# Size classes at the entry of an expert visit, and second products moved behind the join, in a fused attention and mixture-of-experts kernel

## The chip, the cores and the metric

One core of one Trainium2 chip runs the whole program. The metric is the device time of one execution in microseconds; the runs of a kernel are summed up by their median. Five engines work at once, each through its own list of instructions: TensorE (PE in the profile, with its weight loads as PEld), VectorE (DVE), ScalarE (ACT), GpSimd (POOL) and SyncE (SP), which issues DMA. An `If` in the program is a comparison and a branch in the list of every engine.

## The reference

Attention with rotary positions, a gated MLP behind an RMS norm, and then the stage that this change is about, an expert layer that sends each of 2304 tokens to one of 8 experts:

```python
def _moe2_ref(x, modality_id, w_gate, modality_bias, w1, w2):
    logits = x @ w_gate + modality_bias[modality_id]
    e_idx = np.argmax(logits, axis=1)
    ...                                  # probs: softmax of logits
    gate_w = probs[np.arange(N), e_idx]
    out = np.zeros((N, D), dtype=np.float32)
    for e in range(E):
        mask = e_idx == e
        if not mask.any():
            continue
        h = np.maximum(x[mask] @ w1[e], 0.0)
        out[mask] = gate_w[mask, None] * (h @ w2[e])
    return out.astype(np.float32)
```

D is 512, and the hidden width F is 1024. How many tokens an expert gets is known only when the kernel runs.

## The kernel before

Attention and MLP take the first 850 us or so and are not touched. The expert stage is a list of visits. A visit is one expert and up to 384 of its tokens (`VT`); an expert with more gets a further visit. Visit 0 is the fullest expert and is always laid out for 384 tokens, without a branch. Visits 1 to 5 always run, and 6 to 13 stand in nested `If`s on the number of visits (`nvis`); here there are eight visits, 0 to 7. What a visit is (expert, column of the table of tokens, size) VectorE works out while visit 0 runs: `count1` writes the size of visit 1 (`vn1`), `visits` the rest (`vi`). `number` loads such a value into registers, for the size on all engines.

`body` branches on the size: first above 256 or not, then above 288 and above 352, or above 128. Each of the five leaves is a whole visit for 128, 256, 288, 352 or 384 tokens, and after it the engines join and go on with the next visit's load and comparisons. By the column counts in the trace, visits 1 to 7 run as 288, 256, 256, 384, 352, 128 and 352.

A leaf (`visit`, in steps that it yields) makes, for each of eight slices f of the hidden width, 12 products over the transposed tokens `xT` (three for each of four pieces of w1, since values are held as a high and a low part) into one of three banks `ph`; ScalarE applies ReLU into the high part of `hq`, and VectorE subtracts to get the low part. Then come the second products, for each tile of 128 tokens in two halves of 12, into a bank `po`; VectorE scales the tile by its gate into `cvt` (`put`), and GpSimd scatters it to `out`. `small_visit`, for up to 128 tokens, makes the hidden values with tokens as rows in two halves of 12 products, and turns them by transposes (`turn`).

`ahead`, called after each step, puts two kinds of work for the next visit between these: `xT` (four TensorE transposes of a gathered tile of tokens into a bank `pt` or `pc`, a ScalarE cast for the high part, a VectorE subtraction for the low) at the steps that `TURNS` names, and `wsplit` (a weight piece of 512 KB, already loaded by SP, cast by ScalarE and split by VectorE) at the steps that `SPLITS` names; an entry s: n means that after step s all pieces up to 8v + n are split. A visit uses eight pieces, and there are eleven buffers `W`/`Wl`, so that a piece's split waits until the piece eleven before it is used up. `gather` fetches the next visit's tokens by an indirect DMA at the start of a visit. All this is written out in the order in which the engines run it; nothing reorders it later.

Of the kernel before, what the change touches and what calls it, by code (L numbers as in the profile page):

```python
# [9 lines left out]
F32 = mybir.dt.float32  # L10
# [40 lines left out]
class Kernel:  # L51
# [817 lines left out]
YW = 520  # L869
SPLITS = [  # L870
# [4 lines left out]
]  # L875
TURNS = [{}, {8: (0, 1), 9: (2,)}, {8: (0,), 9: (1, 2)}, {8: (0,), 9: (1,), 10: (2,)}]
# [22 lines left out]
class Fused(Kernel):  # L899
# [241 lines left out]
    def count1(self):  # L1141

        V = self.nc.vector
        r = self.rt
        c = r.tile([1, NE], F32, name="c1")
        V.tensor_tensor(c, self.cnt[0:1], self.oh1[0:1], op=ALU.mult)
        n = r.tile([1, 1], F32, name="n1")
        V.tensor_reduce(n, c, axis=AX.X, op=ALU.add)
        self.vn1 = r.tile([1, 1], I32, name="vn1")
        V.tensor_scalar(self.vn1, n, float(VT), None, op0=ALU.min)  # L1150

    def visits(self):
# [52 lines left out]
        V.tensor_scalar(vi[:, 2 * n1:3 * n1], col, 0.0, float(VT), op0=ALU.max, op1=ALU.min)  # L1205


    def moe_open(self):
# [10 lines left out]
        self.rawp, self.wpc, self.ev = {}, {}, {}  # L1219
# [18 lines left out]
    def number(self, v, x, **kw):  # L1238

        n1 = NV - 2  # L1240
        if v < 2:
            t = self.vn1 if x == 2 else self.vi0[0:1, 2 * v + x:2 * v + x + 1]
        else:
            t = self.vi[0:1, n1 * x + v - 2:n1 * x + v - 1]
        return self.nc.values_load(t, min_val=0, max_val=(NE - 1, 141, VT)[x], **kw)
# [62 lines left out]
    def visit(self, v, N):  # L1308
# [19 lines left out]
        for t0 in range(0, N, P):  # L1328
            ps = self.p_o()
            for x in range(2):  # L1330
                self.second(v, ps, x, t0, min(N - t0, P))
                if x == 1:
                    self.put(ps, ix, g, t0 // P, min(N - t0, P))
                yield s
                s += 1

    def small_visit(self, v):
# [28 lines left out]
        ps = self.p_o()  # L1366
        self.second(v, ps, 0, 0, P)
        turn(1)
        yield 8
        yield 9  # L1370
        self.second(v, ps, 1, 0, P)
        self.put(ps, ix, g, 0, P)
        yield 10
        yield 11
# [27 lines left out]
    def ahead(self, v, s, nt=3):  # L1402

        if s >= 8 and v + 1 < NV:
            for t in TURNS[nt].get(s, ()):
                self.xT(v + 1, t, self.p_h if nt == 1 and t == 2 else None)
        i = SPLITS[nt if v else 0]
        if s in i:
            self.wsplit(8 * v + i[s])
# [11 lines left out]
    def body(self, v, n, sizes):  # L1421

        if len(sizes) > 1:
            s = self.state()
            m = len(sizes) // 2
            with self.tc.If(n > sizes[m - 1]) as cmp:  # L1426
                self.body(v, n, sizes[m:])
            self.restore(s)
            with cmp.Else():
                self.body(v, n, sizes[:m])  # L1430
            return
        N = sizes[0]
        if N == P and v + 1 < NV:
            self.gather(v + 1)
        for s in self.visit(v, N) if N > P else self.small_visit(v):
            if s == 0 and N > P and v + 1 < NV:
                self.gather(v + 1)
            self.ahead(v, s, (N + P - 1) // P)

    def moe(self, v):  # L1440
        if v == NV:
            return
        with ExitStack() as es:
# [4 lines left out]
            n = self.number(v, 2)  # L1448
            self.body(v, n, SIZES)
            if v + 1 == NSTAT:  # L1450
                self.nvis = self.nc.values_load(self.vi[0:1, 3 * NV - 6:3 * NV - 5], min_val=2, max_val=NV)
            if v >= NSTAT:
# [15 lines left out]
    def run(self):  # L1468
# [72 lines left out]
        for s in self.visit(0, VT):  # L1541
# [61 lines left out]
```

## Time and profile before

| | |
|---|---|
| runs of the kernel before | 1141.26, 1143.42, 1147.27 us, median 1143.42 |
| the profiled execution | 1141.17 us, of which the profile's span is 1139.4 |
| TensorE busy | 1049.5 us, 92% of the span |
| VectorE, ScalarE, GpSimd busy | 657.6 us (58%), 459.5 (40%), 292.1 (26%) |
| granted TensorE clock, mean | 0.98 |

Times within the span are in us from its start. A busy time of TensorE is the union of its products' intervals; each product is preceded by a weight load that may overlap the product before it. [...] Idle time in brackets is what the engine waited before the row, and for whom; "issue" is time in which it waited for nothing that the profile shows. Rows named PEldq are those of TensorE's sequencer (loads of registers, comparisons and branches), and are not counted as busy.

### The profile page before, as it was taken

Reading aid. Unit: us, or ns where it says so; the run is one execution under the profiler, and the core shown is the slowest. Engines: PE = TensorE matmul, PEld = TensorE weight load, DVE = VectorE, ACT = ScalarE, POOL = GpSimd, SP = SyncE. Lnnn points to the kernel's source line nnn. Section 1 sums busy time; section 2 is a strip of 40 time slices with the busy share of each in tenths; the row PEclk is TensorE's granted clock in tenths of the full one; section 3 lists DMA queues with packets and bytes.
Section 4 is the critical chain, followed back from the end, with each engine's and each line's share of the span. In section 5 each row is a group of like instructions: output and inputs, shape, how many; then the busy total and the mean of one; then the engine's idle time right before and its main releaser. Section 6 shows DMA issues by size and latency. Waiting matters only on the chain. (4 is left out here: it accounts for less than half of the span.)

```text
span 1139.4 us, 19259 instructions
## 1 busy us (share of the span) xinstructions
PE 1049.5 (92%) x7174; PEld 893.3 (78%) x7174; DVE 657.6 (58%) x1308; ACT 459.5 (40%) x1024; POOL 292.1 (26%) x357
## 2 busy tenths in 40 slices
PE   3999999999999899999999999999988879998695
PEld 3776777676776688899999999998877768997583
DVE  8654656676544766556565564553477745663373
ACT  2655555565556333322222222221335434443252
POOL 7553446366302402112011110110010311221211
PEclk9999999999999899999999999999999999999897
DMA  4333344444230201111131111101064755654563
GB/s 131 95 85 89 103 109 130 108 105 129 59 89 24 77 19 58 54 47 47 40 122 47 38 47 47 38 10 56 30 216 156 229 176 169 202 171 140 168 223 122
DMA packets 75993, 114.05 MB, mean 100 GB/s; under 512 B 18536, under 2 KB 43392, under 8 KB 75842
## 3 DMA queue, kind: packets, MB, share of 16 engines
q1 hardware_dynamic: 72162, 100.25, 29.4%
q0 software_dynamic: 3680, 11.91, 3.1%
q8 instruction: 80, 1.31, 0.5%
q14 instruction: 71, 0.58, 0.2%
HBM read 85.91 MB, written 12.17 MB: 86 GB/s over the span
## 5 line engine op out<-in xcount | busy, mean ns | idle before, releaser
L760 PE MATMUL gv<-xh,whi 128*128 128x384 f32 x576 | 197.4, 343 | 1.8 <-ACT xh L738 1.4
L760 PE MATMUL gv<-xl,whi 128*128 128x384 f32 x576 | 195.2, 339 | 3.3 <-POOL xl L742 3.1
L760 PE MATMUL gv<-xh,wlo 128*128 128x384 f32 x576 | 195.2, 339 | 0.4 <-POOL wlo L659 0.4
L293 DVE TENSOR_REDUCE m<-s 128x1 fp32r<-128x576 f32 (+1 forms) x160 | 119.9, 752 | 123.2 <-PE s L292 122.0
L320 ACT ACTIVATE E<-sT 128x576 f32<-128x576 f32 (+1 forms) x160 | 105.0, 659 | 137.9 <-PE sT L319 132.5
L659 POOL TENSOR_TENSOR wlo<-cvt,whi 128x256 fp32r<-128x256 f32 x66 | 50.8, 773 | 339.9 <-ACT whi L658 339.8
L770 DVE TENSOR_TENSOR s<-s,gv 128x384 f32<-128x384 f32 x72 | 39.8, 554 | 154.4 <-PE gv L760 143.6
L760 PEld LDWEIGHTS gv<-xh,whi 128*128 128x128 f32 x576 | 108.9, 189 | 7.9 <-issue 3.5
L760 PEld LDWEIGHTS gv<-xl,whi 128*128 128x128 f32 x576 | 109.2, 190 | 5.4 <-POOL xl L742 3.4
L769 ACT ACTIVATE s<-gv 128x384 f32<-128x384 f32 x72 | 34.9, 492 | 189.6 <-PE gv L760 189.6
L760 PEld LDWEIGHTS gv<-xh,wlo 128*128 128x128 f32 x576 | 109.2, 190 | 1.2 <-POOL wlo L659 1.0
L317 PE MATMUL sT<-qT,kT 128*128 128x288 f32 (+1 forms) x320 | 79.7, 331 | 12.5 <-ACT qT L274 12.4
L788 PE MATMUL yps<-whi,hh 128*128 128x512 f32 x216 | 87.3, 404 | 2.9 <-ACT yacc L793 1.4
L331 PE MATMUL av<-E,vraw 128*64 128x288 f32 x640 | 86.2, 413 | 0.1
L803 DVE TENSOR_TENSOR yacc<-yacc,yps 128x512 f32<-128x512 f32 x99 | 67.6, 685 | 31.9 <-PE yps L788 30.7
L788 PE MATMUL yps<-wlo,hh 128*128 128x512 f32 x216 | 85.3, 395 | 0.0
L788 PE MATMUL yps<-whi,hl 128*128 128x512 f32 x216 | 85.2, 394 | 0.0
L292 PE MATMUL s<-kT,qT 128*128 128x288 f32 (+1 forms) x320 | 78.3, 330 | 6.1 <-DVE m L293 3.8
L1293 POOL DMA_INDIRECT x<-ysc,ix x27 | 32.9, 1218 | 151.2 <-DVE e L1127 76.2
L317 PEld LDWEIGHTS sT<-qT,kT 128*128 128x128 f32 (+1 forms) x320 | 47.9, 181 | 29.3 <-ACT qT L274 20.4
L319 PE MATMUL sT<-qB,kB 65*128 65x288 f32 (+1 forms) x320 | 69.8, 300 | 0.0
L331 PEld LDWEIGHTS av<-E,vraw 128*64 128x64 f32 x640 | 42.7, 137 | 31.6 <-issue 6.5
(288 smaller groups left out, 1979.0 us busy)
## 6 DMA issues: line engine op xcount, KB each, us to landing
raw<-in_w SPq DMA_DIRECT2D x52, 512.0 KB
stt<-in_w SPq DMA_DIRECT2D x26, 512.0 KB
stt<-in_w_gate SPq DMA_DIRECT2D x24, 256.0 KB
stt<-in_w_val SPq DMA_DIRECT2D x24, 256.0 KB
stt<-in_w_out SPq DMA_DIRECT2D x24, 256.0 KB
kB<-kT SPq DMA_DIRECT2D x32, 144.0 KB
qB<-qT SPq DMA_DIRECT2D x32, 144.0 KB
qT<-qT SPq DMA_DIRECT2D x32, 144.0 KB
```

What stands on the lines that cost most here:

```text
L292: nc.tensor.matmul(s[:n, u, 0:288], qA[:, j * 128:j * 128 + n], kA[:, u * 288:u * 288 + 288], start=True, stop=True)
L293: nc.vector.tensor_reduce(m[:n, j:j + 1], s[:n, :, 0:288], axis=AX.XY, op=ALU.max)
L317: nc.tensor.matmul(s[:n, u, 0:288], kA[:, j * 128:j * 128 + n], qA[:, u * 288:u * 288 + 288], start=True, stop=False)
L319: nc.tensor.matmul(s[:n, u, 0:288], kB[0:65, j * 128:j * 128 + n], qB[0:65, u * 288:u * 288 + 288], start=False, stop=True)
L320: nc.scalar.activation(e.rearrange("p (u c) -> p u c", u=2), s[:n, :, 0:288], AF.Exp, scale=0.125)
L331: self.nc.tensor.matmul(av[64 * h:64 * h + 64, 0:288], V[:, h, j * 64:j * 64 + 64], E[:, h if j < 4 else 0, j, 288 * u:288 * u + 288], sta ...
L659: nc.gpsimd.tensor_tensor(lo, f, fr(hi), op=ALU.subtract)
L760: nc.tensor.matmul(t[:, :CH], w[:, k], r[:, k], start=(n == 0), stop=(n == 11))
L769: nc.scalar.activation(s, ps[0][:, :CH], AF.Silu)
L770: nc.vector.tensor_tensor(s, s, ps[1][:, :CH], op=ALU.mult)
L788: nc.tensor.matmul(ps, l, r[:, 2], start=(n == 0), stop=(n == tot - 1))
L803: nc.vector.tensor_tensor(old[:, t], old[:, t], ps, op=ALU.add)
```

## The change

The two parts are these. First, the size is replaced by a class from 0 to 4, which `size_class` makes with one comparison for each of 128, 256, 288 and 352 and adds up; the class of the next visit is loaded at the start of a visit (`size`). `body` compares the class with 3, 2, 1 and 0 in a chain whose next link directly follows, and whose last fall-through is the leaf for 128 tokens; the other leaves are reached by a taken branch. Second, a leaf no longer holds the second products of the first token tile. They stand in `tail`, once, behind the join, together with the three transpositions of the next visit's tokens and two of its weight splits. `SPLITS` and `TURNS` are fitted to that: every leaf ends with the pieces up to 8v + 13 split, the tail brings 14 and 15, and piece 16 falls to the next visit's first step. Visit 0 keeps its order (`SPLIT0`, `first` = 0).

```diff
@@ -867,13 +867,14 @@
+SPLIT0 = {1: 7, 3: 8, 5: 9, 7: 10, 8: 11, 9: 12, 10: 13, 11: 14, 12: 15, 13: 16}
 SPLITS = [
...
-    {1: 9, 3: 10, 5: 11, 8: 12, 9: 13, 10: 14, 11: 15, 12: 16},
+    {},
+    {0: 9, 5: 11, 9: 13},
+    {0: 8, 1: 9, 3: 10, 5: 11, 8: 12, 9: 13},
+    {0: 8, 1: 9, 3: 10, 5: 11, 8: 12, 10: 13},
 ]
-TURNS = [{}, {8: (0, 1), 9: (2,)}, {8: (0,), 9: (1, 2)}, {8: (0,), 9: (1,), 10: (2,)}]
+TURNS = {8: (0,), 9: (1,), 10: (2,)}
@@ -1147,7 +1148,15 @@
-        V.tensor_scalar(self.vn1, n, float(VT), None, op0=ALU.min)
+        self.size_class(self.vn1, n, r.tile([1, 1], F32, name="sc1"))
+
+    def size_class(self, o, n, t):
+
+        V = self.nc.vector
+        V.tensor_scalar(t, n, float(SIZES[0]), None, op0=ALU.is_gt)
+        for x in SIZES[1:-2]:
+            V.scalar_tensor_tensor(t, n, float(x), t, op0=ALU.is_gt, op1=ALU.add)
+        V.scalar_tensor_tensor(o, n, float(SIZES[-2]), t, op0=ALU.is_gt, op1=ALU.add)
@@ -1202,7 +1211,7 @@
-        V.tensor_scalar(vi[:, 2 * n1:3 * n1], col, 0.0, float(VT), op0=ALU.max, op1=ALU.min)
+        self.size_class(vi[:, 2 * n1:3 * n1], col, r.tile([1, n1], F32, name="sc2"))
@@ -1325,7 +1334,8 @@
         s = 8
-        for t0 in range(0, N, P):
+        st["last", v] = ix, g
+        for t0 in range(first, N, P):
@@ -1363,15 +1373,26 @@
-        ps = self.p_o()
-        self.second(v, ps, 0, 0, P)
         turn(1)
+        st["last", v] = ix, g
         yield 8
         yield 9
+
+    def tail(self, v):
+
+        ix, g = self.st.pop(("last", v))
+        ps = self.p_o()
+        more = v + 1 < NV
+        if more:
+            self.xT(v + 1, 0)
+            self.wsplit(8 * v + 14)
+            self.xT(v + 1, 1)
+        self.second(v, ps, 0, 0, P)
+        if more:
+            self.xT(v + 1, 2)
+            self.wsplit(8 * v + 15)
         self.second(v, ps, 1, 0, P)
         self.put(ps, ix, g, 0, P)
-        yield 10
-        yield 11
@@ -1418,24 +1439,35 @@
-    def body(self, v, n, sizes):
...
+    def size(self, v):
+        if v not in self.cls:
+            self.cls[v] = self.number(v, 2)
+        return self.cls[v]
+
+    def body(self, v):
+
+        s = self.state()
+
+        def arm(x):
+            N = SIZES[x]
...
+        def choose(x):
+            if x == 0:
+                arm(0)
+                return
+            with self.tc.If(self.size(v) > x - 1, preferred_fallthrough_block=False) as cmp:
+                arm(x)
             self.restore(s)
             with cmp.Else():
-                self.body(v, n, sizes[:m])
...
+                choose(x - 1)
+
+        choose(len(SIZES) - 1)
@@ -1445,10 +1477,12 @@
-            n = self.number(v, 2)
-            self.body(v, n, SIZES)
+            for x in range(v, min(v + 2, NV)):
+                self.size(x)
+            self.body(v)
             if v + 1 == NSTAT:
                 self.nvis = self.nc.values_load(self.vi[0:1, 3 * NV - 6:3 * NV - 5], min_val=2, max_val=NV)
+            self.tail(v)
```

How this lies on the engines is seen best at the entry of visit 1 and at the join behind it. In these rows a line number, an operation, its output and inputs by tile (with buffer numbers) and its shape follow each other; `vn` and `vi` are the sizes, `po` the banks of second products, `ph` those of the first, `W` and `Wl` weight pieces. TensorE's list at the entry of visit 1, before:

```order
L1394 MATMUL po_8984<-Wl_8966,hq 128x512 x6
L1245 TENSOR_LOAD vn_9184
L1426 COMPARE_AND_BRANCH x3
L1319 MATMUL ph_8982<-xT,Wl_8967 128x384 x3
L1319 MATMUL ph_8982<-xT,Wl_8968 128x384 x3
```

and now, where four comparisons stand in a row, the sizes of two visits are loaded, and the leaf for 128 tokens follows instead of that for 384:

```order
L1415 MATMUL po_8984<-Wl_8966,hq 128x512 x6
L1254 TENSOR_LOAD vn_9184
L1254 TENSOR_LOAD vi
L1464 COMPARE_AND_BRANCH x4
L1367 MATMUL po_8985<-Wl_8967,xT 128x512 x3
L1367 MATMUL po_8985<-Wl_8968,xT 128x512 x3
```

At the join of visit 1, TensorE's list before goes from a leaf's last second product straight to the load and the comparisons:

```order
L1394 MATMUL po_8984<-W_8654,hq 128x512
L1426 UNCONDITIONAL_BRANCH
L1245 TENSOR_LOAD vi
L1426 COMPARE_AND_BRANCH x3
L1319 MATMUL ph_8982<-xT,Wl_8964 128x384 x3
```

Now the tail stands between the join and them: the transposes (L1312) of the next visit's tokens, and the second products of the first tile around the last of these:

```order
L1312 MATMUL pt_6361<-idf,x_8664 128x128 x4
L1415 MATMUL po_8984<-W_8651,hq 128x512 x6
L1415 MATMUL po_8984<-W_8652,hq 128x512 x6
L1312 MATMUL pc_6362<-idf,x_8665 128x128 x4
L1415 MATMUL po_8984<-W_8653,hq 128x512 x6
L1415 MATMUL po_8984<-W_8654,hq 128x512
L1415 MATMUL po_8984<-W_8655,hq 128x512
L1415 MATMUL po_8984<-W_8654,hq 128x512 x2
L1415 MATMUL po_8984<-W_8655,hq 128x512
L1415 MATMUL po_8984<-W_8654,hq 128x512
L1254 TENSOR_LOAD vi
L1464 COMPARE_AND_BRANCH x4
```

ScalarE's list at the same join, before, at the end of the leaf for 256 tokens: casts of the next visit's tokens (L1305) and of weight pieces (L1277) take turns, and all of them are in the leaf.

```order
L1305 CAST xT<-pc_6362 128x4x128
L1277 CAST Wl_8967<-raw_8647 128x1024
L1277 CAST Wl_8968<-raw_8648 128x1024
L1305 CAST xT<-pt_6361 128x4x128
L1305 CAST xT<-pc_6362 128x4x128
L1277 CAST Wl_8969<-raw_8649 128x1024
L1277 CAST W_8650<-stt 128x1024
L1277 CAST W_8651<-stt 128x1024
L1426 UNCONDITIONAL_BRANCH
```

Now the three casts of tokens (L1314) and two of weight pieces (L1286) have moved behind the branch, and the last piece has gone to the next visit:

```order
L1286 CAST Wl_8967<-raw_8647 128x1024
L1286 CAST Wl_8968<-raw_8648 128x1024
L1464 UNCONDITIONAL_BRANCH
L1314 CAST xT<-pc_6362 128x4x128
L1286 CAST Wl_8969<-raw_8649 128x1024
L1314 CAST xT<-pt_6361 128x4x128
L1314 CAST xT<-pc_6362 128x4x128
L1286 CAST W_8650<-stt 128x1024
L1254 TENSOR_LOAD vi
L1464 COMPARE_AND_BRANCH x4
```

## Rows read from the trace of the kernel before

**Rows 1.** TensorE in time: start, us, operation, out and in, shape, count, [idle].

```profile
886.57 0.66 PE L1303 MATMUL pt<-idf,x 128*128 128x128 f32 x4 [2.67 <-DMA x<-ysc,ix]
...
902.49 1.45 PE L1319 MATMUL ph<-xT,Wl 128*128 128x288 f32 x9 [0.71 <-issue]
...
939.08 6.18 PE L1319 MATMUL ph<-xT,Wl 128*128 128x256 f32 x34 [5.78 <-issue]
...
967.27 0.98 PE L1319 MATMUL ph<-xT,W 128*128 128x256 f32 x3 [2.27 <-issue]
...
992.60 0.69 PE L1319 MATMUL ph<-xT,Wl 128*128 128x384 f32 x3
...
1031.30 0.91 PE L1319 MATMUL ph<-xT,Wl 128*128 128x352 f32 x4 [4.08 <-issue]
...
1076.07 1.19 PE L1357 MATMUL po<-W,xT 128*128 128x512 f32 x2 [9.62 <-issue]
```

**Rows 2.** Branches of TensorE's sequencer (L1426): count, min/median/max ns, first and last start.

```profile
L1426 PEldq COMPARE_BRANCH  x2: 92/2107/4122, 898.2 to 898.3; - x2
...
L1426 PEldq COMPARE_BRANCH  x1: 4360/4360/4360, 929.0 to 929.0; - x1
...
L1426 PEldq COMPARE_BRANCH  x1: 4957/4957/4957, 933.8 to 933.8; - x1
...
L1426 PEldq COMPARE_BRANCH  x2: 306/2852/5399, 960.8 to 961.6; - x2
...
L1426 PEldq COMPARE_BRANCH  x1: 3725/3725/3725, 1027.5 to 1027.5; - x1
...
L1426 PEldq COMPARE_BRANCH  x2: 3303/4287/5271, 1067.3 to 1072.6; - x2
...
L1426 PEldq COMPARE_BRANCH  x1: 347/347/347, 1089.5 to 1089.5; - x1
```

**Rows 3.** The load of a size on TensorE's sequencer (L1245), same columns.

```profile
L1245 PEldq TENSOR_LOAD <-vi x1: 312/312/312, 933.4 to 933.4; - x1
```

**Rows 4.** TensorE in time, the last products of visit 1 and of visit 6.

```profile
924.40 0.60 PE L1303 MATMUL pc<-idf,x 128*128 128x128 f32 x4
924.75 8.55 PE L1394 MATMUL po<-W,hq 128*128 128x512 f32 x36
...
1089.74 1.53 PE L1394 MATMUL po<-W,hq 128*128 128x512 f32 x6
```

**Rows 5.** TensorE's comparison with the number of visits, behind visit 6 (L1443).

```profile
L1443 PEldq COMPARE_BRANCH  x1: 70/70/70, 1088.7 to 1088.7; - x1
```

**Rows 6.** Stretches: length, busy us of PE, PEld, DVE, ACT, POOL, PEclk, DMA, GB/s.

```profile
885.00:889.00 4.00, 2.43 (x13) 2.10 (x14) 2.07 (x7) 1.54 (x2) 1.55 (x1) 1.00 0.81 287
936.60:943.20 6.60, 4.12 (x19) 4.15 (x20) 0.42 (x1) 0.38 (x1) 0.00 (x0) 0.50 0.05 9
967.30:970.50 3.20, 3.20 (x15) 3.20 (x16) 0.00 (x0) 0.16 (x1) 1.00 (x1) 0.50 0.86 312
1032.20:1035.40 3.20, 3.20 (x13) 3.20 (x12) 0.27 (x1) 0.46 (x1) 0.00 (x0) 0.50 0.04 13
1069.70:1079.80 10.10, 3.73 (x9) 2.99 (x10) 1.50 (x3) 0.00 (x0) 3.67 (x4) 0.50 0.46 152
```

**Rows 7.** VectorE in time: the last operation that writes the sizes.

```profile
897.79 0.16 DVE L1205 TENSOR_SCALAR vi<-col 1x12 int32<-1x12 f32 x1
```

**Rows 8.** ScalarE in time, in visit 6: a weight piece, then the second ReLU.

```profile
1084.15 1.06 ACT L1277 CAST W<-stt 128x1024 fp32r<-128x1024 f32 x1
1085.10 0.60 ACT L1362 ACTIVATE x<-po 128x512 f32<-128x512 f32 x1
```

**Rows 9.** ScalarE's casts of tokens (L1305): count, min/median/max ns, first and last start.

```profile
L1305 ACT CAST xT<-pc x13: 586/587/596, 918.7 to 1117.4; 128x512 fp32r<-128x512 f32 x13
```

**Rows 10.** VectorE in time: the last scaling of a tile.

```profile
1125.64 0.75 DVE L1398 TENSOR_SCALAR cvt<-po,g 96x512 f32<-96x512 f32 x1 [1.84 <-PE po L1394]
```

**Rows 11.** GpSimd in time: the last scatter.

```profile
1129.09 0.92 POOL L1400 DMA_INDIRECT out<-cvt,ix  x1 [6.22 <-DMA out<-cvt,ix]
```

More of the change, by code (lines that the diff above doesn't have):

```diff
@@ L1218, in moe_open @@
         self.g_x = Ring(m, 3, [P, YW], F32, "x")
-        self.rawp, self.wpc, self.ev = {}, {}, {}
+        self.rawp, self.wpc, self.ev, self.cls = {}, {}, {}, {}
         self.nld = self.nsp = 0
@@ L1244, in number @@
             t = self.vi[0:1, n1 * x + v - 2:n1 * x + v - 1]
-        return self.nc.values_load(t, min_val=0, max_val=(NE - 1, 141, VT)[x], **kw)
+        return self.nc.values_load(t, min_val=0, max_val=(NE - 1, 141, len(SIZES) - 1)[x], **kw)
     def expert(self, v):
@@ L1306, in xT, with visit @@
         nc.vector.tensor_tensor(l, ps, fr(h), op=ALU.subtract)
-    def visit(self, v, N):
+    def visit(self, v, N, first=P):
         nc, st = self.nc, self.st
@@ L1402, in ahead @@
     def ahead(self, v, s, nt=3):
[L1404 to L1407, printed above, removed]
+        if v == 0 and s >= 8:
+            for t in TURNS.get(s, ()):
+                self.xT(1, t)
+        i = SPLITS[nt] if v else SPLIT0
         if s in i:
@@ L1419, in restore @@
         self.nld, self.nsp = s[4:]
-    def body(self, v, n, sizes):
[L1423 to L1427, printed above, removed]
+    def size(self, v):
[6 more added lines that the diff above has]
+            N = SIZES[x]
+            if N == P and v + 1 < NV:
+                self.gather(v + 1)
+            for y in self.visit(v, N) if N > P else self.small_visit(v):
+                if y == 0 and N > P and v + 1 < NV:
+                    self.gather(v + 1)
+                self.ahead(v, y, (N + P - 1) // P)
+        def choose(x):
[4 more added lines that the diff above has]
+                arm(x)
             self.restore(s)
             with cmp.Else():
-                self.body(v, n, sizes[:m])
[L1431 to L1438, printed above, removed]
+                choose(x - 1)
+        choose(len(SIZES) - 1)
     def moe(self, v):
@@ L1540, in run @@
         self.wsplit(6)
-        for s in self.visit(0, VT):
+        for s in self.visit(0, VT, 0):
             if self.rq:
```

3 rows, old and new, of the table SPLITS are left out of this document.

## The prediction

> **What bounds the kernel now.** I read the page's shares first, then TensorE's own order of time over the expert visits, then what its sequencer did in the holes, then the granted clock there. TensorE is busy for most of the span, so only its idle time and its slow time are worth anything, and of both the expert visits hold nearly all that a change of branches can touch. Visit 0 has a fixed size; by the column counts of the products, the seven visits behind it run as 288, 256, 256, 384, 352, 128 and 352 tokens. [Rows 1] show the first product of six of them (from 902.49 on), and the idle time before it: 0.71, 5.78, 2.27, none, 4.08 and 9.62 us. The releaser is "issue": nothing that the profile shows was being waited for. The seventh (352) waits only for VectorE, which I leave out. The sum is 22.46 us.
>
> The sequencer's branches say what it was [rows 2]. A comparison that falls through takes 0.09 us (0.13 with the gap behind it, an estimate), a jump to near code 0.31 or 0.35, and a jump to far code 3.3 to 5.4. The same jump, over the 384 arm into the 352 arm, took 3.73 us at 1027.5 and 0.35 at 1089.5; the first came just after another far jump, the second after a long straight run. So what is near depends on what has been fetched, not on the distance alone. The seven far jumps shown take 4.12, 4.36, 4.96, 5.40, 3.73, 3.30 and 5.27 us, a mean of 4.4. Before the jump stands the load of the size, 0.31 us and about 0.1 around it [rows 3].
>
> TensorE does not stop when its sequencer does. The exit branch of visit 1 began at 929.0, while the last 36 products ran from 924.75 to 933.30 [rows 2, 4]: the sequencer was 4.3 us ahead, some 18 products of 0.2375 us (8.55 / 36). Such a lead pays for one far jump, not for two. This is the pattern of [rows 1]: no jump, no idle; one, 0.71 or 2.27; two, 4.08 or 5.78; three (128 tokens), 9.62.
>
> The clock makes it dearer. [...] A wait of 2.67 us at 886.57 (for a gather) left it at 1.00 [rows 1, 6].
>
> So the visits lose 22.5 + 7.1 = 29.6 us, and the last one is followed by a wait on POOL.
>
> **The change, part by part.** The order shows that the change does what it says: a visit now costs TensorE one far jump in and at most one out, with 24 products and 12 transposes standing between the two. Those are 24 x 0.2375 + 12 x 0.09 = 6.8 us of work (four transposes start 0.35 us before what follows them [rows 4]), and no product is added or dropped.
>
> *Jumps out.* A lead of 4.3 us stands against 4.4: 0.2 us per miss. By the lengths of the arms (242 to 289 instructions of TensorE, a product being two) the arms of 256 and 288 come out onto near code, so three exits miss (384, 352, 352): 0.6 us. The small arm's exit is below.
>
> *Jumps in.* Behind the join, the queue holds at best the last 18 entries: 12 products, 4 transposes, 2 products, 12 x 0.2375 + 0.35 + 0.45 = 3.6 us. Against it stand the load of a size 0.41 (now that of the next visit, but still on the path), the comparisons that fall through at 0.13 each, the jump 4.4 and 0.05 until the first product. The two visits of 256 tokens (three comparisons fall through): 0.41 + 0.39 + 4.4 + 0.05 - 3.6 = 1.65 us each. The visits of 352 (one falls through; the last also tests the count of visits): 1.4 and 1.5. 384 tokens: its arm begins 70 instructions behind the first comparison, near code, 0.35 us, hidden. 128 tokens: falls straight in, hidden.
>
> *Visit 1* gets worse. It has no second products ahead of it (visit 0 keeps its order), and all engines now also load the size of visit 2, which VectorE finishes at 897.95 [rows 7]. The class adds four tiny operations there, and four for visit 1 earlier; at the 0.16 us of that row plus a gap, 0.8 us. So the load can start at 898.75, ends at 899.2, two comparisons 0.26, the jump 4.4: first product at 903.9. TensorE ran dry at 902.49 - 0.71 = 901.78: 2.1 us, where it lost 0.71.
>
> *The small visit (128)* gets a new wait. Its hidden tiles are turned by transposes that need the second ReLU. Today 12 second products stand before the second turn and cover it; now they are in the tail. The ReLU starts directly behind a weight cast of 1.06 us and takes 0.60 [rows 8]: 1.66 us in which TensorE has nothing. The jump out is 4.4 us but starts while the first products are still queued, so I take it as hidden behind this. The next visit's gather had the hole of 9.62 us to land in; now its rows are wanted some 9 us after the visit begins: 0.8 us more. Together 2.5, between 0 and 6.9 (2.5 with the whole jump behind it).
>
> *Moved casts.* The next visit's tokens are transposed, cast and split in the tail instead of between second products. The last transposes start some 3.2 us before the tail ends (twelve products and themselves), the cast takes 0.59 [rows 9] and VectorE's subtraction about as much, and the cast of a weight piece (1.06) stands before it. I price it at nothing: this slack covers it, and if the cover is gone it is a rival below. The weight splits are the same eight per visit; two stand in the tail. SP's loads follow the splits as before.
>
> *The end.* The last copy to `cvt` starts at 1125.64 but its scatter only at 1129.09, held by the landing of the scatter before [rows 10, 11]. After the change that one has the tail's 6.8 us to land. The 3.45 us between the two shrink to 2 at best about 1; I take 1.5 us gained.
>
> *Clock.* Six idle times of 1.4 to 2.5 us are left. 2.27 us brought the low clock once, 2.67 did not; half of six at 1.65 us: 5 us.
>
> **Sum.** After: 0.6 + 2 x 1.65 + 1.4 + 1.5 + 2.1 + 2.5 = 11.4, and 5 for the clock, 16.4 us. Saved: 29.6 - 16.4 + 1.5 = 14.7. The profiled execution took 1141.17 us, so 1126.5; the median of the runs, 1143.42, lies 2.25 above that execution, so 1128.7. I say 1128.5.
>
> [...]
>
> **Rivals.**
> *B: the queue hides the jumps in wholly.* If the lead behind the join is over 5.3 us, the jumps in cost nothing. Left are visit 1 (2.1), the small visit (2.5) and one low clock (1.65): 6.3; saved 29.6 - 6.3 + 1.5 = 24.8: 1118.5. For it: an exit that nearly vanishes, 0.71 at visit 1. Against it: every lead that I can read is 4.3 or less. [...] [Rows 4] show 4.3.
> *C: the queue is not full again by the end of the tail.* The small visit's sequencer left at 1088.7 while its products ran to 1089.74 + 1.53 = 1091.27 [rows 4, 5]: 2.6 us ahead only. With that, each of four jumps in costs 1.0 more, and all six idle times bring the low clock: 15.4 + 9.9 = 25.3; saved 5.8: 1137.6.
> *D: slower.* If the sequencer stands still at the tail's transposes until TensorE reaches them, there is no lead behind the join. The jumps in then cost 3.6 more each (20.6), the small visit's exit is open too (6.9), with 2.7 for visit 1 and the exits 30.2, and six low clocks at 1.9 make 41.6: 12.0 more than today, less the 1.5 of the end: 1153.9. It turns to the slow side where the lead is under about 1.2 us. For it: 2.6 us at the small visit. Against: elsewhere 4.3, past many waiting products.
> *E: the casts end last.* If ScalarE or VectorE enter the tail late, each visit starts some 1.5 us later: six of them, 9 us of the forecast's gain given back: 1137.5. For it: they do a whole visit's eight splits in less time. Against: at none of the six entries of [rows 1] are they what is waited for.
>
> **Chances.** Forecast 0.53, B 0.12, C 0.17, D 0.06, E 0.12. Half a per cent, 5.7 us, is about what a measurement of this kernel tells from no change, so faster means under 1137.7: nearly all of the forecast's share, all of B, half of C and E: 0.77. Within: 0.17. Slower: D, 0.06. The range for 8 in 10 goes from 1116 (B, with shorter jumps) to 1141 (C and E).
>
> **What would show it.** In the new trace: one far branch of about 4.4 us at each entry but those of 384 and 128, with 1 to 2.5 us idle behind it; at visit 1 more idle than the 0.71; nothing like 9.62 before 128 tokens, but a wait for the ReLU and a gather inside that visit; the clock at 0.50 in fewer stretches. Idle over 3 us at the entries of 256 would make C or D right; the first product of a visit waiting for VectorE or ScalarE would make E right.

## The result, and the profile after

The changed kernel takes 1131.33 us (median of 4 runs, 1129.5 to 1134.08), the kernel before 1142.35 on the same chip (4 runs). The ratio, here and below that of the means, is 0.9897, with a 95% interval from 0.986 to 0.9935. A second set of 6 runs, beside other kernels, gave 0.9912 (0.9889 to 0.9935). The profiled execution took 1130.2 us, with a span of 1128.4.

TensorE in time in the changed kernel, the rows that answer to [rows 1]; the idle time stands in brackets:

```profile
903.39 1.47 PE L1328 MATMUL ph<-xT,Wl 128*128 128x288 f32 x9 [1.07 <-issue]
...
937.28 2.85 PE L1328 MATMUL ph<-xT,Wl 128*128 128x256 f32 x22 [2.61 <-issue]
941.06 7.19 PE L1328 MATMUL ph<-xT,Wl 128*128 128x256 f32 x59 [0.93 <-issue]
...
965.38 1.31 PE L1328 MATMUL ph<-xT,W 128*128 128x256 f32 x9 [2.96 <-issue]
...
1026.27 6.03 PE L1328 MATMUL ph<-xT,Wl 128*128 128x352 f32 x36 [1.81 <-issue]
...
1067.43 0.66 PE L1357 MATMUL ph<-idf,x 128*128 128x128 f32 x4 [1.71 <-ACT x L1372]
1073.53 1.08 PE L1312 MATMUL pt<-idf,x 128*128 128x128 f32 x4 [5.44 <-issue]
...
1082.75 9.56 PE L1328 MATMUL ph<-xT,W 128*128 128x352 f32 x58 [0.72 <-issue]
```

The 9.62 us before 128 tokens are gone and the entries are down to 0.7 to 3 us. But inside the small visit there are now 1.71 us for the ReLU and, behind its second turn (the four transposes of its second half of hidden values), a hole of 5.44 that no visit had before. With 0.17 us at 907.14 the idle time of visits 1 to 7 is 17.4 us, where it was 23.0 (22.46, and the 0.54 before visit 7).

The branches of TensorE's sequencer (L1464), which answer to [rows 2], in the same columns; entries, with the exits of visits 4 (1013.3), 5 (1048.6) and 6 (1067.4):

```profile
L1464 PEldq COMPARE_BRANCH  x2: 64/2743/5422, 931.6 to 931.7; - x2
L1464 PEldq COMPARE_BRANCH  x2: 64/2934/5805, 959.3 to 959.4; - x2
L1464 PEldq COMPARE_BRANCH  x1: 358/358/358, 986.1 to 986.1; - x1
L1464 PEldq COMPARE_BRANCH  x1: 3847/3847/3847, 1013.3 to 1013.3; - x1
L1464 PEldq COMPARE_BRANCH  x2: 81/2556/5032, 1021.0 to 1021.2; - x2
L1464 PEldq COMPARE_BRANCH  x1: 3278/3278/3278, 1048.6 to 1048.6; - x1
L1464 PEldq COMPARE_BRANCH  x4: 64/64/72, 1056.5 to 1056.8; - x4
L1464 PEldq COMPARE_BRANCH  x1: 5924/5924/5924, 1067.4 to 1067.4; - x1
L1464 PEldq COMPARE_BRANCH  x1: 3841/3841/3841, 1078.9 to 1078.9; - x1
```

The far jumps out at 1013.3 and 1048.6 leave no idle time at all. The one at 1067.4 starts in the moment in which the second turn starts, and lasts until the hole ends (1067.43 + 5.92 = 1073.35).

The load of a size (L1254), which answers to [rows 3], and the last second products of visit 1 in TensorE's time, which answer to [rows 4]:

```profile
L1254 PEldq TENSOR_LOAD <-vi x1: 317/317/317, 930.9 to 930.9; - x1
```

```profile
931.68 2.99 PE L1415 MATMUL po<-W,hq 128*128 128x512 f32 x12
```

TensorE ran dry, that is, ended the last product that it had, at 934.67 (the first product of visit 2 less its idle time); the load began at 930.89. That is a lead of 3.78 us.

Stretches behind three holes, which answer to [rows 6] in the same columns:

```profile
937.00:946.00 9.00, 7.80 (x64) 7.62 (x65) 4.57 (x9) 4.46 (x8) 3.77 (x3) 1.00 0.51 160
965.00:974.00 9.00, 8.62 (x72) 8.65 (x73) 5.83 (x11) 4.73 (x8) 4.38 (x4) 1.00 0.52 155
...
1069.70:1073.50 3.80, 0.00 (x0) 0.00 (x1) 2.36 (x2) 0.95 (x2) 0.00 (x0) 0.50 1.03 343
1073.50:1076.50 3.00, 2.97 (x11) 2.75 (x12) 0.94 (x2) 1.81 (x3) 0.00 (x0) 0.50 0.73 289
```

The holes of 2.61 and 2.96 us left the granted clock, a share of full speed, at 1.00. Only behind the hole in the small visit does TensorE work at 0.50: 3.0 us, of which half, 1.5, is counted as lost; before, 7.4 were. The half is an estimate from the share: in the trace of the kernel before, the products of 256 columns at the start of visit 2 begin 0.213 us apart at 0.50 and 0.120 apart at 1.00.

The last scaling on VectorE and the last scatter on GpSimd, which answer to [rows 10, 11]:

```profile
1116.58 0.75 DVE L1419 TENSOR_SCALAR cvt<-po,g 128x512 f32<-128x512 f32 x1
```

```profile
1117.61 0.99 POOL L1421 DMA_INDIRECT out<-cvt,ix  x1 [5.03 <-DVE cvt L1419]
```

The scatter follows 1.03 us behind the start of the scaling, where it took 3.45. Behind the last product the kernel now takes 11.9 us; before it was 13.8.

When visit 1 begins differs from one profiled execution to the next by up to 4.7 us (TensorE runs dry before it between 898.4 and 903.0 us), and no edit here changes what TensorE does ahead of it. So profiles are compared from that moment on. In the table, in us, idle is TensorE's idle time from that moment to its last product, low clock is its busy time at 0.50 times a half, and the last column goes from that moment to the end of the span. The ratios are those of all runs; the other columns are read from one profiled execution of each kernel.

| kernel | ratio to before (95%) | idle | low clock | behind the last product | from dry to the end |
|---|---|---|---|---|---|
| before | 1 | 23.0 | 7.4 | 13.8 | 237.6 |
| changed | 0.9897 (0.9860 to 0.9935) | 17.4 | 1.5 | 11.9 | 226.1 |
| changed, second set | 0.9912 (0.9889 to 0.9935) | 18.9 | 4.5 | 11.8 | 230.2 |
| chain alone | 0.9981 (0.9950 to 1.0013) | 22.1 | 6.9 | 13.7 | 237.0 |
| tail alone | 0.9881 (0.9836 to 0.9925) | 15.0 | 3.9 | 12.0 | 224.2 |
| arms reordered | 0.9879 (0.9830 to 0.9927) | 10.0 | 2.7 | 12.2 | 221.2 |
| turn without its wait | 0.9890 (0.9842 to 0.9938) | 14.6 | 5.8 | 11.4 | 226.5 |
| third turn early | 0.9851 (0.9814 to 0.9889) | 13.7 | 3.2 | 11.3 | 223.4 |
| size loaded early | 0.9872 (0.9840 to 0.9903) | 15.3 | 3.3 | 11.7 | 225.4 |
| gather and casts | 0.9932 (0.9896 to 0.9968) | 15.5 | 6.2 | 16.6 | 232.9 |
| a quarter of the weights | 0.9815 (0.9780 to 0.9849) | 10.8 | 3.0 | 11.0 | 219.8 |
| all edits | 0.9798 (0.9773 to 0.9822) | 5.6 | 3.0 | 15.2 | 218.9 |
| gather in the arms | 0.9809 (0.9784 to 0.9834) | 8.8 | 3.4 | 12.4 | 220.6 |
| gather left | 0.9837 (0.9810 to 0.9864) | 10.1 | 3.4 | 12.4 | 221.0 |

From before to changed, idle, low clock and the end fall by 5.6, 5.9 and 1.9 us, 13.4 in all, and the last column by 11.5. The other 1.9 us went to products that took a little longer and to gaps too short to count as idle, spread over the visits; why is not shown. Most of the variants can't be told from the changed kernel by their times, since the intervals overlap; what they show is read from their traces. Only the chain alone lies above the changed kernel in both of its sets, and only a quarter of the weights, all edits and gather in the arms lie below.

### The profile page after: what moved, and what is told of

The parts are those of the page before. It is cut to its first block, busy times and chain, and to the rows that moved or that the text cites. A ratio compares the mean times of both kernels' runs of the same rounds, so it can differ in the third digit from the quotient of the medians.

```text
span 1128.4 us, 19271 instructions
## 1 busy us (share of the span) xinstructions
PE 1048.8 (93%) x7174; PEld 891.2 (79%) x7174; DVE 655.5 (58%) x1313; ACT 457.5 (41%) x1023; POOL 293.2 (26%) x357
```

## The experiments

In these edits `...` marks lines left out; they are against the changed kernel, but for that of the tail alone. An arm is a leaf of a visit's branches.

**The two halves of the change, each alone.** The chain alone:

```diff
...
-        for t0 in range(first, N, P):
+        for t0 in range(0, N, P):
...
-            self.tail(v)
...
```

> The chain alone: the class of size, its early load and the compact chain are kept, all second products stand in the arms again with the weight splits and turns of the kernel before. Theory (TensorE's idle time at a visit's entry is its far jumps less a queue lead of about 4 us, wherever they come from): an exit and an entry are next to each other again. Entries of visits 1 to 7: 1.1, 2.6, 3.0, 0 (near exit, near arm), about 5 (far exit of 384, far jump to 352), about 0.3 (far exit, fall into 128), about 7 (far exit of 128 with a short lead, far jump to 352): 19 us, and two low clocks, 3 us. Of the kernel before that is 29.6, so some 8 us faster than before, ratio about 0.993, slower than the changed kernel by some 3 us. Rival 1 (the tail is the whole gain): the chain alone is the kernel before, 1.000. Rival 2 (the chain is the whole gain): 0.990.

TensorE's sequencer in it (L1451: the exit of visit 4, then the entry of visit 5), and the first products of visits 5 and 7:

```profile
L1451 PEldq COMPARE_BRANCH  x1: 3695/3695/3695, 1015.7 to 1015.7; - x1
L1451 PEldq COMPARE_BRANCH  x2: 81/3194/6306, 1020.0 to 1020.1; - x2
```

```profile
1026.46 0.95 PE L1327 MATMUL ph<-xT,Wl 128*128 128x352 f32 x2 [6.43 <-issue]
...
1086.44 0.96 PE L1327 MATMUL ph<-xT,W 128*128 128x352 f32 x2 [8.76 <-issue]
```

Measured: 0.9981, no change that can be told. The idle time was forecast at 19 and came to 22.1; the low clock, forecast at 3, cost 6.9. The first rival holds. With exit and entry next to each other, two far jumps (3.70 and 6.31 us between visits 4 and 5) stand against one lead, and the chain mostly moves the holes to other visits.

The tail alone, against the kernel before:

```diff
...
-        for t0 in range(0, N, P):
+        st["last", v] = ix, g
+        for t0 in range(first, N, P):
...
+            self.tail(v)
...
```

> The tail alone: the sizes are loaded and compared in the tree of the kernel before, with its layout of arms (384, 352, 288, 256, 128), and only the second products of the first token tile stand behind the join. Theory: one jump in per visit, two for 128 tokens; the small arm now lies directly before the join, so its exit costs nothing. Idle of visits 1 to 7: 0.7, 1.9, 1.9, 0, 1.5, 5.6 at the entry of 128, then 1.7 for the ReLU and 0.5 for the gather in it, 0.9: 14.7 us, with one low clock 16.6. The changed kernel has 17.4 and 1.5. So about 2 us faster than the changed kernel, ratio to before about 0.988. Rival (the chain carries the gain): about 1.000. A tail that is worth no more than the chain alone would come out at 0.993 or above.

The sequencer at the entry of visit 6 (L1439), and that visit's first product:

```profile
L1439 PEldq COMPARE_BRANCH  x2: 3818/4588/5358, 1050.7 to 1056.1; - x2
```

```profile
1060.11 1.19 PE L1359 MATMUL po<-W,xT 128*128 128x512 f32 x2 [6.17 <-issue]
```

Measured: 0.9881, as expected. Its idle time was forecast at 14.7 and is 15.0, its low clock at 1.9 and is 3.9. The tree still pays two jumps before 128 tokens (6.17), but its small arm lies directly before the join and pays none behind. So all of the gain that can be told is the tail's. Beside it the chain is worth nothing that can be told: the intervals of both kernels lie over each other.

**The hole behind the small visit's turn.** In the first run the second turn reads what is ready:

```diff
-    nc.tensor.transpose(ps[:, k], hs[x][:, k * P:(k + 1) * P], self.idf)
+    nc.tensor.transpose(ps[:, k], hs[0][:, k * P:(k + 1) * P], self.idf)
```

> The changed kernel, but the small visit's second turn reads the half of the hidden values that the first turn read, so it doesn't wait for the second ReLU (left out: the 128-token visit's second half of hidden values isn't used). Theory A (the sequencer can't reach the jump out while a transpose in front of it waits for the ReLU, so the jump starts with no lead): the 1.71 us go, the jump starts up to 4 us before TensorE runs dry, and the hole of 5.44 us shrinks to the landing of the next visit's gathered tokens, about 3 us in all where 7.15 are: ratio to before about 0.986, 4 to 5.5 us faster than the changed kernel. Rival 1 (the jump is long for its own sake, behind a full queue of transfers, and starts late whatever stands before it): only the 1.7 us go, 0.988. Rival 2 (the hole is the gather's): 0.9897, no change.

The exit of visit 6 in it, and TensorE around it:

```profile
L1464 PEldq COMPARE_BRANCH  x1: 3799/3799/3799, 1064.0 to 1064.0; - x1
```

```profile
1066.33 0.60 PE L1357 MATMUL ph<-idf,x 128*128 128x128 f32 x4
1069.46 0.83 PE L1312 MATMUL pt<-idf,x 128*128 128x128 f32 x4 [2.53 <-DVE g L1406]
1071.45 1.08 PE L1312 MATMUL pc<-idf,x 128*128 128x128 f32 x4 [1.16 <-DMA x<-ysc,ix]
```

The jump now begins at 1064.00, 2.3 us before the turn that it used to wait for, and is over at 1067.80, 0.87 us after TensorE ran dry (1066.93). The rest waits for gathered tokens. Those of the first tile, issued at 1063.62, landed 5.70 us later, at 1069.32, and the sequencer's wait for them ended at once; the row names VectorE, whose operation ended at 1069.37. 7.15 us became 3.69, as theory A has it (about 3). The time can't show it: the interval of 0.989 holds all three forecasts, and the profiled execution lost 4 us more to the low clock (5.8, where the changed kernel's profile has 1.5).

The second run leaves the turn's wait and takes away the other suspects:

```diff
-    {0: 9, 5: 11, 9: 13},
+    {0: 11, 9: 13},
...
             self.wsplit(8 * v + 15)
+        if v + 2 < NV:
+            self.gather(v + 2)
...
```

> The changed kernel with two edits to what the small visit waits for: the gather of the next visit's tokens stands in the tail of the visit before, ahead of its last scatter, and the two weight casts that ScalarE does just before the second ReLU are done at the start of the visit. Theory: the wait for the ReLU falls from 1.71 to about 0.7 us; the jump out still starts only when the second turn's wait ends, so the hole behind it stays at about 5 us although the gathered tokens now lie ready: ratio to before about 0.989, 1 to 2 us faster than the changed kernel. Rival (the hole was the gather's): it goes, 0.984.

The exit of visit 6; TensorE there; and GpSimd at the end of the program:

```profile
L1466 PEldq COMPARE_BRANCH  x1: 7154/7154/7154, 1065.6 to 1065.6; - x1
```

```profile
1065.61 0.66 PE L1357 MATMUL ph<-idf,x 128*128 128x128 f32 x4 [0.69 <-ACT x L1372]
1072.94 1.09 PE L1312 MATMUL pt<-idf,x 128*128 128x128 f32 x4 [6.67 <-issue]
```

```profile
1120.63 1.00 POOL L1302 DMA_INDIRECT x<-ysc,ix  x1 [0.30 <-issue]
1121.93 1.02 POOL L1423 DMA_INDIRECT out<-cvt,ix  x1 [0.30 <-issue]
```

The wait for the ReLU fell to 0.69 as expected, the hole stayed and ended with the jump (1065.61 + 7.15 = 1072.76): it is the jump's, not the gather's. The tokens for these transposes had landed at 1064.1, those of the third tile only at 1072.4, so without the jump a wait for these was to be expected next. But the kernel reads slower than the changed one, 0.9932 against the expected 0.989, though their intervals overlap. What had been left out: behind the last visit the tail now issues three gathers for a visit that doesn't come, ahead of the last scatter, and 4.7 us more stand behind the last product (16.6).

**Where a jump's target lies.** The arms in another order, nothing else:

```diff
+ARMS = (3, 4, 2, 0, 1)
...
-    with self.tc.If(self.size(v) > x - 1, preferred_fallthrough_block=False) as cmp:
-        arm(x)
+    with self.tc.If(self.size(v) == o[0], preferred_fallthrough_block=False) as cmp:
+        arm(o[0])
...
```

> The changed kernel with its arms in another order: 256 tokens are fallen into, then 352, 384, 288, and 128 directly before the join. No instruction of a visit is changed. Theory (a jump costs by where its target lies, and a queue lead of 3.8 us stands against it): entries of 256 free (they cost 2.6 + 0.9 and 3.0), of 352 a near jump and free (1.8 and 0.7), of 384 now a far jump, 1.6; 288 as it is, 1.1; 128 with four comparisons and a far jump, 2.1, but out of it no jump: the 5.44 us hole behind its second turn is gone and the 1.7 us for the ReLU stay. 6.5 us idle where the changed kernel has 17.4, one low clock less: about 12 us faster than the changed kernel, ratio to before about 0.979. Rival 1 (taken branches cost alike wherever they go, or the order of tests matters): 0.990, as the changed kernel. Rival 2 (the hole behind the small visit's turn is the wait for the gathered tokens of the next visit, not the jump): the hole of 5 us stays, 0.984.

The branches (L1465): entry of visit 2 (256), its exit, entries of visits 4 (384) and 5 (352); then TensorE at the entry of visit 2 and behind the small visit's turn:

```profile
L1465 PEldq COMPARE_BRANCH  x4: 63/63/75, 927.0 to 927.4; - x4
L1465 PEldq COMPARE_BRANCH  x1: 5118/5118/5118, 942.8 to 942.8; - x1
L1465 PEldq COMPARE_BRANCH  x2: 75/2386/4698, 977.2 to 977.4; - x2
L1465 PEldq COMPARE_BRANCH  x1: 379/379/379, 1014.3 to 1014.3; - x1
```

```profile
930.15 3.10 PE L1329 MATMUL ph<-xT,Wl 128*128 128x256 f32 x25
...
1062.86 1.09 PE L1313 MATMUL pt<-idf,x 128*128 128x128 f32 x4 [1.32 <-DMA x<-ysc,ix]
```

The entries came out as forecast: 256 and 352 free, 384 now 1.45 (1.6), 128 1.93 (2.1), 288 0.88 (1.1). The hole of 5.44 is gone. Two things had been left out: the exits of the two visits of 256 are now far and long (5.1 and 5.0 us), and leave 1.00 and 0.83; and behind the turn the gathered tokens are waited for, 1.32 and 0.92. The low clock stayed. 10.0 us idle instead of 6.5, 4.9 us less from dry to the end than the changed kernel where 12 were expected; the ratio, 0.9879, can't be told from the changed kernel's.

**What the lead is.** The third turn (the transposes of the third tile of the next visit's tokens) ahead of all second products of the tail:

```diff
             self.xT(v + 1, 1)
+            self.xT(v + 1, 2, self.p_h)
         self.second(v, ps, 0, 0, P)
         if more:
-            self.xT(v + 1, 2)
```

> The changed kernel with the third turn of the next visit's tokens moved ahead of all second products of the tail (into a bank of the first products' ring), so the last 18 entries of the queue are 18 products of 512 columns, where 12 products, 4 transposes and 2 products stand today. Theory (the lead is a count of queued entries, some 18 pairs of weight load and product): the lead at the entries of visits 2, 3, 5 and 7 rises from 3.8 us to 4.3, their idle time falls by 0.5 each, 2 us in all; ratio to before about 0.988. Rival 1 (the lead is a time of about 3.8 us, or is set by what the transposes wait for): no change, 0.9897. Rival 2 (three casts at the start of the tail come late and the third turn waits for the join): slower than the changed kernel by 1 to 3 us, 0.992.

The load of a size at the entry of visit 2, and TensorE there:

```profile
L1254 PEldq TENSOR_LOAD <-vi x1: 317/317/317, 927.6 to 927.6; - x1
```

```profile
926.06 5.72 PE L1415 MATMUL po<-W,hq 128*128 128x512 f32 x24
932.45 0.83 PE L1328 MATMUL ph<-xT,Wl 128*128 128x256 f32 x5 [0.66 <-issue]
```

TensorE ran dry at 931.79, 4.23 us after the load began (927.56). At visits 3, 5 and 7 it is 4.30, 4.32 and 4.20, where the changed kernel has 3.79, 3.85 and 3.72. At visits 2, 3 and 5 of both kernels the trace has the same 19 products unfinished when the load begins, the running one among them. So the lead is a count of entries, some 18 products with their weight loads, and not a time. The ratio is 0.9851, 0.003 better than expected. These 18 products are 36 instructions with their weight loads, and no run shows a longer lead.

Loading the size of the next visit in the tail instead of in front of the comparisons:

```diff
         self.second(v, ps, 0, 0, P)
         if more:
+            self.size(v + 1)
...
-            for x in range(v, min(v + 2, NV)):
-                self.size(x)
+            self.size(v)
...
```

> The changed kernel with the load of the next visit's size moved from that visit's predecessor's entry into the tail, between its two halves of second products. Theory (the terms of an entry add up: load, comparisons, jump, less the lead): each of the entries of visits 2, 3, 5 and 7 loses the 0.41 us of the load, visit 1 the 0.4 of the second load: 2 us in all, ratio to before about 0.988. Rival (the load in the tail holds the sequencer up there, so the queue is no fuller at the branch): no change, 0.9897.

Measured: 0.9872 (expected 0.988), which can't be told from the changed kernel. The first product of visit 1 waits 0.51 us instead of 1.07, visit 5 none instead of 1.81; visit 3 has 3.42, because its jump took 6.5 us this time. What the load is worth is less than the scatter of one jump.

**Why jumps are long.** From visit 2 on only a quarter of the expert weights is brought:

```diff
-                self.nc.sync.dma_start(r, src)
+                q = 1024 if v < 2 else 256
+                self.nc.sync.dma_start(r[:, 0:q], src[:, 0:q])
...
```

> The changed kernel, but from visit 2 on each piece of the expert weights brings only the first quarter of its columns (left out: the rest of these weights; the casts and products run as before, on what lies in the buffer). Theory (a far jump's code comes over the same DMA engines as the weights, so transfers lengthen it): the jumps of visits 2 to 7, 3.3 to 5.9 us in the changed kernel (mean 4.6), all come near 3.4; the idle time at visits 2, 3, 5 and 7 falls by 1 to 2 us each, the hole behind the small visit's turn from 5.4 to about 3.3: some 7 us in all, ratio to before about 0.983. Rival (a jump's length is set by the distance or by the blocks that its target spans, or by the other engines' jumps at the same time): the jumps stay at 3.3 to 5.9 us in the same places, 0.9897.

Entries of visits 2 and 3 and the exit of visit 6 (L1466):

```profile
L1466 PEldq COMPARE_BRANCH  x2: 64/1833/3602, 928.6 to 928.7; - x2
L1466 PEldq COMPARE_BRANCH  x2: 64/2093/4122, 954.6 to 954.7; - x2
L1466 PEldq COMPARE_BRANCH  x1: 4234/4234/4234, 1059.9 to 1059.9; - x1
```

They were 5.42, 5.80 and 5.92. All far jumps of visits 2 to 7 now lie between 3.35 and 4.23 us, and the ratio is 0.9815 (0.983 expected). So the weights' transfers made these jumps longer, by 1.7 to 1.8 us in the three shown.

The trace of the changed kernel has the fetch itself. These are transfers that began during the exit of visit 5 (1048.61 to 1051.89), then during that of visit 6 (1067.43 to 1073.36): queue and kind, packets, MB, share of the time of 16 engines.

```profile
q1 hardware_dynamic: 54, 0.22, 34.3%
q8 instruction: 1, 0.02, 1.8%
```

```profile
q1 hardware_dynamic: 640, 1.54, 76.8%
...
q8 instruction: 1, 0.02, 1.2%
```

A packet of 16384 bytes on q8 begins within each of the 133 far jumps of TensorE in the fourteen profiles, and within none of the five near jumps (0.29 to 0.36 us) in those of the kernel before and the changed one; by its kind and its times it carries the code that the jump waits for. In these two it took 0.96 and 1.09 us, and both jumps ended 1.3 us after it had landed; but it began 0.98 us after the start of the first jump and 3.49 us after that of the second. Over the 123 jumps with all weights, the time until the last such packet begins goes from 0.4 to 4.8 us (median 1.4), while the packet's own has a median of 1.0; with a quarter of the weights the former is 1.0 to 1.9. So what the weights lengthen is mostly the time until the code's packet begins: in the two jumps above it began after 0.98 us where the kernel's own transfers on q1 took 34.3% of the engines' time, and after 3.49 where they took 76.8%.

**Together.** Reordered arms, early third turn, early size, casts ahead of the ReLU, gather in the tail.

> All of these together: the arms in the order 256 (fallen into), 352, 384, 288, 128; the third turn early; the next size loaded in the tail; the gather in the tail; the casts ahead of the ReLU. Theory: the terms add up. Idle: visit 1 0.5, the far exits of the two visits of 256 0.9 each, 384 0.5, 128 1.0, the ReLU 0.7, no wait for the gather: some 4.5 us where the reordered arms alone have 10.0, and no low clock in the visits (2.8 less): some 8 us faster than the reordered arms, ratio to before 0.980. Rival (what is freed at one wait is lost at the next, the casts or the weight loads): as the reordered arms, 0.987.

TensorE behind the small visit's turn:

```profile
1061.83 1.09 PE L1313 MATMUL ph<-idf,x 128*128 128x128 f32 x4 [2.67 <-DVE Wl L1288]
```

Measured: 0.9798, 1119.11 us, the fastest version. It beats both kernels: its interval (to 0.9822) lies under that of the changed kernel in either set. It is not all as expected: the third turn waits 2.67 us, and 15.2 us stand behind the last product, for the same gathers as above. The row names VectorE for the 2.67 us, but its split ended at 1061.83, when the turn's weight load had already begun (1061.80). The gather of the third tile, issued at 1053.73, landed 7.96 us later, at 1061.69, and the sequencer's wait for it ended with that. So the turn waited for gathered tokens, although their gather now stands in the tail of the visit before. The order of the arms is made for these sizes.

Two attempts to get these back, of which the first took the row at its word. The gather moved into the arm, and the third turn behind six products:

> The arms reordered, the next size loaded in the tail, the casts ahead of the ReLU, as in the version with all edits; the gather of the next but one visit now stands in the arm, two steps behind the gates, so nothing stands ahead of the last scatter; the third turn stands behind six second products, so that 18 products still follow it and it comes 1.4 us later to the bank that VectorE must free. Theory: the time behind the last product goes back from 15.2 us to about 12, and the wait of 2.67 us in the small visit to about 1.2: 4 to 5 us faster than the version with all edits, ratio to before about 0.976. Rival (the gather's three descriptors cost VectorE or POOL as much in the arms): 0.980, as that version.

The time behind the last product did fall to 12.4, but in place of the 2.67 us a second product behind the turns waits 3.34 us, this time for VectorE (its split ended at 1065.71, the product began at 1065.76), and the arm of 384 had a jump of 5.9 us. 0.9809, no better. The gather left where the changed kernel has it:

> The version with all edits but without moving the gather: arms reordered, third turn early, next size loaded in the tail, casts ahead of the ReLU. Theory: the time behind the last product goes back from the 15.2 us of the version with all edits to about 12, and what the gather makes the small visit wait lies beside the 2.67 us for VectorE there: some 3 us faster than that version, ratio to before 0.977. Rival (the tokens of the visit behind the small one now come later than VectorE's casts): 1 to 2 us of it are lost again, 0.979.

TensorE behind the small visit's turn:

```profile
1063.28 1.11 PE L1313 MATMUL pc<-idf,x 128*128 128x128 f32 x4 [3.56 <-DMA x<-ysc,ix]
1067.04 1.09 PE L1313 MATMUL pt<-idf,x 128*128 128x128 f32 x4 [2.64 <-DMA x<-ysc,ix]
```

0.9837: the rival, and more of it; the tokens come 6.9 us late in all (with 0.66 for the third turn). The changed kernel ran once more on the chip of the second version:

> The changed kernel once more, beside the last version on one chip: 0.990 of the kernel before.

Its rows are in the table.

## Why the prediction was right, and where it was not

The forecast was 1128.5 us, 2.8 below the median, and inside its own case: far jumps less a lead of about 4 us. It saved 14.9 us of a median of 1143.42, where 11.0 of 1142.35 were measured.

- **Jumps out**: 0.6 forecast, none measured. The exits were 3.3 to 3.9 us, shorter than the mean of 4.4 that I took, since few weights move at that point (DMA share 0.31 to 0.39 at their start). Of the exits taken as near, that of the arm of 288 took 0.29 us (923.54), and the two visits of 256 show no exit branch; whether the length of an arm decides this, no run shows.
- **Jumps in**: the sum has the right terms. At visit 2: load and three comparisons 0.80 (forecast 0.80), jump 5.42 (4.4), 0.17 until the first product (0.05), lead 3.78 (3.6): 2.61. What was mis-sized is the jump: at these entries it begins among transfers (DMA share 0.65, 1.01 and 0.84 in its first 2.5 us). 2.61 and 2.96 instead of 1.65, 1.81 instead of 1.4; the last entry, 0.72 instead of 1.5, had a jump of 3.84. The sign set for C or D, over 3 us idle at the entries of 256, was nearly met (2.96, and 3.26 in the second set), but by the jump's length: the lead was full. A further 0.93 us inside visit 2 was not foreseen. 384 and 128 came free, as forecast.
- **Visit 1**: 1.07 instead of 2.1. The second load began 3.36 us before TensorE ran dry (898.96 and 902.32), where 3.03 were forecast, so the class was not dearer than its price; and the jump took 3.67 instead of 4.4.
- **The small visit**: the wait for the ReLU is 1.71 (1.66 forecast). The step that failed is this: "The jump out is 4.4 us but starts while the first products are still queued, so I take it as hidden behind this." It is not hidden: the turn's transposes stand in front of it, and TensorE's sequencer didn't pass them until the ReLU was there (both began at 1067.43). The 2.5 us became 7.15, just over the upper bound of 6.9. Taking the wait away let the jump start 2.3 us ahead of that turn; making the wait shorter, with the turn still waiting, did not shrink the hole. This is rival D's mechanism at one place of the program. At the other entries the sequencer went past the tail's transposes and had its full lead (3.7 to 3.85 us).
- **Moved casts**: nothing, as forecast; no entry waits for ScalarE or VectorE. In the fastest version VectorE ends last at two second products, for 0.26 and 0.53 us.
- **The end**: 1.9 us, forecast 1.5.
- **Clock**: 5 forecast, 1.5 in the first profile and 4.5 in the second. Holes of the same place and nearly the same length (2.96 and 3.26 us, at visit 3) left the clock at 1.00 in one and at 0.50 in the other. One execution differs from the next by 3 us, and two are too few to call the half of six right or wrong. The 7.1 us that the sum takes for the low clock of the kernel before are half of TensorE's busy time in the stretches of [rows 6] at 0.50; all its time at 0.50 in the visits of the same trace gives 7.4. No run shows the half itself: by the products' pace (0.213 us against 0.120) a little less is lost.

Idle 6 us too low and the clock 3.5 too high cancel in part, so the forecast was closer than its terms, and that is luck: in the second profile idle is 7.5 us over the forecast and the clock 0.5 under it.

## What to carry to other kernels

A branch of TensorE cost here what its jump took less what was queued in front of it and not yet run (at visit 2 a jump of 5.42 us, 0.97 around it and a lead of 3.78 left 2.61 idle), so put work that all arms share between the exit and the next entry, with the longest instructions last (the lead at visit 2 rose to 4.23 us) and nothing in front of the branch that must wait for another engine (7.15 us idle in the small visit, 3.69 without that wait). Count the gain per jump, not per comparison: the shape of the chain was worth nothing that can be told here, the order of the arms took 14.5 us of idle time away and brought 7.5 of another kind. Before moving a gather or a cast into code that every visit runs, look at the last visit, which runs it for nobody. Where a row names an engine for a wait, compare its end with the start of what waited, and look at the landing of the data too.

## What the runs showed of the hardware

- The lead of TensorE's sequencer is a count: some 18 products with their weight loads, 3.7 to 3.85 us with four transposes among them and 4.2 to 4.3 with none.
- The sequencer did not pass a transpose whose data another engine still owed: the jump out of the small visit began with the turn (1067.43, after a wait of 1.71 us), and 2.3 us ahead of it once that wait was gone.
- A far jump takes 3.3 to 7.15 us (one took 2.9). Of 123 far jumps in the thirteen profiles with all weights, the 19 that began while the DMA engines were busy for less than 0.35 of their first 2.5 us took 3.28 to 3.86 us (median 3.46), the 10 at 0.95 or more 4.37 to 7.15 (median 5.67).
- Behind some jumps TensorE runs dry again (0.93 us at 941.06; 1.11 and 1.47 in the second set; in visits of 288 and 256). The traces say that the code behind the landing came late: in all 13 holes that end with "issue" elsewhere than at the end of a far jump, a further q8 packet had landed 1.2 to 1.6 us before the hole ended (1.43 at 941.06). No run changed this on purpose.
